# Attention rows as 64-column products on halves of TensorE's rows, all four row blocks at one place of the second layer

## The chip, the core and the metric

The kernel runs on one core of a Trainium2 chip. A core has TensorE (matrix products, with a queue PE for the products and PEld for the loads of their stationary operand), VectorE (DVE), ScalarE (ACT), GpSimd (POOL) and SyncE (SP, which here only issues DMAs). Products are written to PSUM, in eight banks of 128 partitions by 512 floats; all other tiles lie in SBUF. The metric is the time of one execution on the device in microseconds (us). Before the change the median of three runs is 261.56 us.

## What is computed

Eight batches of a linear attention are followed by one feed-forward block over all 8 x 576 tokens:

```python
kv  = einsum('bhsd,bhse->bhde', k, v)      # (8, 8, 64, 64)
out = einsum('bhsd,bhde->bhse', q, kv)     # (8, 8, 576, 64)
rms = sqrt(mean(out * out, axis=-1) + 1e-6)
x   = (out / rms * g_norm)                 # -> (4608, 512), heads side by side
h   = x @ w_in                             # (4608, 2048)
g   = h * sigmoid(1.702 * h)
y   = g @ w_out                            # (4608, 512)
```

The inputs are float32; the products take float16 operands and add up in float32.

## The kernel before

**Token tiles.** The 576 tokens of a batch are cut into 512 tokens, which make one token tile, and 64, which are collected from all batches into a ninth tile. The last loop of the kernel (line 958) runs over the nine tiles `t`. Within a tile the attention of batch `b = t + 1` is interleaved with the two layers of tile `t`. Both layers use a scheme with seven products in place of eight for a two-by-two split of the operands (`SevenIn` for the first layer, `Seven` for the second).

**The second layer.** `Seven.run` (line 670) issues the seven products in the order 1, 5, 6, 2, 7, 3, 4. Each has two row blocks (`mo`) of eight matmuls (`i`) with 256 columns: 112 matmuls, and their running number `n` is the *place* of this text. Product 1 is places 0 to 15, product 5 is 16 to 31, product 6 is 32 to 47, product 2 is 48 to 63, product 7 is 64 to 79, product 3 is 80 to 95 and product 4 is 96 to 111. Products 1, 6, 7 and 4 add up in one PSUM bank, products 5 and 3 in another, product 2 has one from the pool `ps_a`. When product 1, 5 or 6 is complete, ScalarE copies the bank to SBUF (`keep`, line 647), ahead of the next product in that bank; these are the first, second and third copy. Products 2, 7 and 3 end with an addition on VectorE (`place`, line 655), product 4 with a copy. The stationary operands of products 5, 6, 7 and 3 are sums formed on VectorE (`sums`, line 610).

**What is hung on places.** The kernel's order is written out by hand. A `Plan` lists the steps of the first layer, the sums, and at which place of the second layer each step of the attention is called (`units2`, built at lines 1021 to 1031). A step called at a place is issued right after that matmul, on whichever engines it uses, and each engine works through its own queue in that order. Tile 1 uses the plan `SECOND` (attention of batch 2); tiles 2 to 6 use `LATER` (batches 3 to 7). The plan's last products of the first layer can be left for the second: product 4 of the last part, the *late product*, is issued at place 15 in `LATER` and at place 5 in `SECOND`, with its gate on ScalarE (line 538) behind it.

**The attention of batches 2 to 7** (`class Attention`, line 210):

- `kv_product` (line 232) forms K^T V with 40 matmuls whose outputs are 64 by 64; the two heads of a pair go to the two halves of the PSUM partitions, by turns.
- `keep_kv` (line 262) copies them into `kvd`, per head pair a matrix of 128 by 128 whose two diagonal blocks hold the two halves' operands and whose other blocks are zero.
- `transpose_q` (line 270) brings q into `qTd` by a transposing DMA on SP: 128 partitions hold two token blocks of 64 head dimensions each, one above the other.
- `rows(i)` (line 303), for i = 0 to 3: four matmuls of 128 columns with `qTd` as stationary operand and the block-diagonal `kvd` as moving one, into one PSUM bank `outR`; then ScalarE squares the bank into `sq` (line 318). Each of the four banks holds two token blocks for four of the eight heads. The first three banks are from the pool `ps_h`, the fourth is from `ps_a`; there are three buffers of `sq`.
- `add_up(j)` (line 321) sums the squares over 64 columns on VectorE (line 324), `roots(h)` (line 331) takes the inverse root of two such sums on ScalarE (line 333), after a load of the activation table (line 966).
- `turn(j)` (line 335) multiplies the bank by the roots on VectorE (line 337) into `x16`, and after every second one SP issues a transposing DMA (line 346) into the next token tile's operand `xT`.
- `out`, `ss` and `apply` at the fixed places 46, 74 and 80 treat the last 64 tokens in another way: `out` has four matmuls of 64 columns (line 286).

At the start of the next tile the first layer needs `xT`, and from the fifth step on also the differences `xS` (line 490), which VectorE forms from both transposed parts.

The lines of the step that the change rewrites:

Of the kernel before, what the change touches and what calls it, by code (L numbers as in the profile page):

```python
# [7 lines left out]
F16 = mybir.dt.float16  # L8
F32 = mybir.dt.float32
ALU = mybir.AluOpType  # L10
AFT = mybir.ActivationFunctionType

P = 128
# [3 lines left out]
def kernel(  # L17
# [10 lines left out]
    nc = tc.nc  # L28

    B, H, S, D = q.shape  # L30
    DM = H * D
# [5 lines left out]
    SM = 512  # L37
    J = SM // P
# [12 lines left out]
    attn = ctx.enter_context(tc.tile_pool(name="attn", bufs=4))  # L51
# [4 lines left out]
    ps_a = ctx.enter_context(tc.tile_pool(name="ps_a", bufs=3, space=bass.MemoryType.PSUM))  # L56
    ps_h = ctx.enter_context(tc.tile_pool(name="ps_h", bufs=3, space=bass.MemoryType.PSUM))
# [88 lines left out]
    for n in "kqv":  # L146
        if n != "q":
            rows = stage.tile([P, 6, 2 * P], F32, name="qf", tag="qf", bufs=2)
            rows = rows.rearrange("p h x -> p (h x)")[0:PE_]
# [50 lines left out]


    xT = {}

    def scale_w_in(i0, i1):

        for i in (i0, HF + i0):
            w = w_in_sb[:, :, i * P : (i + i1 - i0) * P]
            nc.vector.tensor_scalar_mul(w, w, g_col)

    class Attention:  # L210
# [91 lines left out]

        def rows(self, i):

            pool, tag = (ps_h, "hT") if i < 3 else (ps_a, "att")
            t = pool.tile([P, DM], F32, name="outR", tag=tag)
            for k in range(H // 2):
                h = i % 2 * (H // 2) + k
                nc.tensor.matmul(  # L309
                    t[:, k * P : (k + 1) * P],  # L310
                    self.qTd[:, h * (J // 2) + i // 2, :],
                    self.kb[:, h // 2, :, 1 - h % 2, :],
                    start=(k == 0),
                    stop=True,
                    skip_group_check=True,
                )
            sq = attn.tile([P, SM], F16, name="sq", tag="sq", bufs=3)
            nc.scalar.activation(sq, t, AFT.Square)
            self.o[i] = (t, sq)

        def add_up(self, j):
            if j == 0:
# [10 lines left out]
            nc.scalar.activation(s4, s4, AFT.Abs_reciprocal_sqrt, bias=eps_t, scale=1.0 / D)  # L333

        def turn(self, j):
            j0, c0 = j // 2 * 2, j % 2 * (DM // 2)
            nc.vector.tensor_mul(
                self.x16[:, j0 : j0 + 2, c0 : c0 + DM // 2].rearrange("p l (h d) -> p h l d", d=D),
                self.o[j][0].rearrange("p (h l d) -> p h l d", l=2, d=D),
                self.sum4[:, j, :]  # L340
                .rearrange("p (h l) -> p h l", l=2)
                .unsqueeze(3)
                .to_broadcast([P, H // 2, 2, D]),
            )
            if j % 2:
                nc.sync.dma_start_transpose(
                    out=self.x[:, (j - 1) * KO : (j + 1) * KO, :],
                    in_=self.x16[:, j - 1 : j + 1, :].rearrange("p j n -> p (j n)"),
                )
# [407 lines left out]
    def layers(t, units1, units2):  # L757
        hid = d0 if t == 0 else Hidden(t)
        seven = Seven(t, hid.gT) if t else None
        left = hid_seven(t, hid, seven, units1) if t else first_columns(hid, units1)  # L760
        osbs[t] = opool.tile([P, 4, DM], F32, name="osb", tag="osb")
        if t:
            todo = {n: [lambda x=x: seven.sums(*x) for x in xs] for n, xs in plan(t).later.items()}
            for n, us in units2.items():
                todo.setdefault(n, []).extend(us)
            for n, us in left.items():
                todo[n] = us + todo.get(n, [])
            seven.run(todo)
        else:
            project_all(hid.gT, units2)  # L770
        if t < EARLY:
            store_early(t)
        elif t < B and t not in HALVED:
            store(t, 0, J)
# [81 lines left out]
    for hl in range(2):  # L856
        r = slice(hl * D, (hl + 1) * D)
# [34 lines left out]
    for fo in COLS[4:GROUP]:  # L892
# [25 lines left out]
        "ahoh",  # L918
        {5: '34'},
        (-1, 0, 0, 4),  # L920
        {'rows': (0, 2, 8, 19), 'add_up': (6, 26, 27, 31), 'table': 26, 'roots': (27, 33), 'turn': (40, 50, 51, 52)},
    )
    LATER = Plan(
# [7 lines left out]
        "aahh",  # L931
        {15: '34'},
        (0, 1, 6, 11),
        {'rows': (1, 1, 3, 15), 'add_up': (2, 18, 27, 22), 'table': 24, 'roots': (28, 39), 'turn': (35, 38, 46, 48)},
    )
    LAST_TWO = Plan(
# [12 lines left out]
    def plan(t):  # L949
        return SECOND if t < EARLY else LATER if t < B - 1 else LAST_TWO  # L950
# [7 lines left out]
    for t in range(NT):  # L958
        b = t + 1
        u1, u2 = {}, {}  # L960

        def at1(i, f, *args):
            u1.setdefault(i, []).append(lambda: f(*args))

        def at2(i, f, *args):
            u2.setdefault(i, []).append(lambda: f(*args))  # L966

        def of(b, name, *args):
            return lambda: getattr(live[b], name)(*args)

        if t == 0:
            for l in range(2):
                at1(6, nc.vector.memset, kvd[l], 0.0)
            at1(7, of(0, "out", NPAIR))
            at1(7, scale_w_in, 0, 4)
            at1(7, w_in_sums, 0, 2)
            at1(8, start, 1)
            at1(12, scale_w_in, 4, 6)
            at1(12, w_in_sums, 2, 3)
            at1(13, load_q, 2)  # L980
            at2(4, setattr, a0, "ss_pool", Attention.ss_pool)
            at2(4, of(0, "ss", NPAIR, True))
            at2(4, of(0, "apply", NPAIR))
            at2(18, weight_sum, 0, 0, HF)
            at2(18, scale_w_in, 6, 8)
            at2(18, w_in_sums, 3, 4)
            for c in range(NPAIR):
                at1(12, of(1, "pack_q", c))
                at2(9 + 3 * c, of(1, "q", c))
                at2((36, 37, 49, 50)[c], of(1, "kv", c))  # L990
                at2((41, 43, 54, 55)[c], of(1, "out", c))
                at2((45, 50, 58, 60)[c], of(1, "ss", c))
                at2((48, 52, 58, 62)[c], of(1, "apply", c))
            for n in range(1, 4):
                at2(19, weight_sum, n, 0, 4)
                at2(38, weight_sum, n, 4, 6)
            at2(39, load_kv, 2, 0, H // 2, False)
            at2(51, clear_rest)
            at2(51, load_kv, 2, H // 2, H)

            def first_sum():
                made[1] = Sums(1, xT[1])
                made[1].form(0)

            at2(55, first_sum)
        elif b < B:
            todo = plan(t)
            at1(todo.steps.index("kv"), of(b, "kv_all", todo.keep))
            if t == 1:
                at1(5, start, b)  # L1010
                at1(5, of(b, "transpose_q"))
                at1(4, nc.scalar.preload_act_table_set, "gelu_apprx_sigmoid_and_others")
                for n, i in ((1, 8), (2, 11), (3, 16)):
                    at1(i, weight_sum, n, 6, HF)
            if t + 2 < B:
                late = max(15, todo.steps.index("kv") + 1)
                at1(late, load_kv, t + 2)
                at1(late, load_q, t + 2)
                at2(100, start, t + 2)
                at2(100, of(t + 2, "transpose_q"))  # L1020
            at = todo.attn
            at2(at["table"], nc.scalar.preload_act_table_set, "abs_reciprocal_sqrt_and_small")
            for h in range(2):
                at2(at["roots"][h], of(b, "roots", h))
            for j in range(J):
                for name in ("rows", "add_up", "turn"):
                    at2(at[name][j], of(b, name, j))
            at2(46, of(b, "out", NPAIR))
            at2(74, of(b, "ss", NPAIR))
            at2(80, of(b, "apply", NPAIR))  # L1030
            at2(82, nc.scalar.preload_act_table_set, "gelu_apprx_sigmoid_and_others")
        elif t < B:
            for name in ("ss_pool", "rest_pool"):
                at2(16, setattr, live[1], name, (ps_a, "att"))
            at2(16, of(1, "out", NPAIR))
            at2(34, nc.scalar.preload_act_table_set, "abs_reciprocal_sqrt_and_small")
            at2(44, of(1, "ss", NPAIR))
            at2(50, of(1, "apply", NPAIR))
            at2(52, nc.scalar.preload_act_table_set, "gelu_apprx_sigmoid_and_others")
        layers(t, u1, u2)  # L1040
# [30 lines left out]
```

## Time and profile before

| | |
|---|---|
| runs of before | 261.62, 261.56, 261.07 us; median 261.56 us |
| the profiled execution | span 259.2 us from its first to its last instruction; the page gives no other time of this execution, so what lies around the span is 2.4 us against the median |
| TensorE | 251.8 us busy in products, 2500 products |
| VectorE, ScalarE, GpSimd | 194.7, 174.9, 53.6 us busy |
| granted TensorE clock | 0.998 over the span |
| row products (line 309) | 96, of which 16 belong to each of batches 2 to 7 |
| squares of the rows (line 318) | 24, 0.600 us each |
| sums of the squares (line 324) | 24, 0.679 us each |
| multiplications (line 337) | 24, 0.684 us each |

The profile is one execution seen by the hardware profiler. *Groups* gather the instructions of a line with their number, busy time and mean duration, and behind the bar the idle time of the engine just before them. *Waits* say who waited for whom, for how long and how often. The *chain of work* follows the end of the kernel back to what released each step; in order of time its rows give start, length and what ran. The *timeline* lists the instructions of an engine in order of time, equal neighbours merged. A product's duration is its latency (273 ns for 256 columns); products follow each other much closer than that.

### The profile page before, as it was taken

What the parts mean: (1) busy time and instruction counts of PE and PEld (TensorE: products, weight loads), DVE (VectorE), ACT (ScalarE), POOL (GpSimd) and SP (SyncE); (2) the same over time, 40 slices, a digit from 0 to 9 for tenths busy, and PEclk for the clock granted to TensorE, in tenths of its full rate; (3) what the DMA queues carried; (4) which work ended last, traced back from release to release, by engine and by line L of the source; (5) the groups of instructions that cost most, each with busy time, mean ns of one, the idle gap of its engine ahead of it and who ended that gap; (6) DMA issues with size and microseconds to landing.
All of it is one profiled execution on the core that took longest, in us unless ns stands there. A gap on an engine that the chain in (4) does not pass through costs nothing.

```text
span 259.2 us, 6157 instructions
## 1 busy us (share of the span) xinstructions
PE 251.8 (97%) x2500; PEld 206.3 (80%) x2500; DVE 194.7 (75%) x351; ACT 174.9 (67%) x315; POOL 53.6 (21%) x81
## 2 busy tenths in 40 slices
PE   8799999999999999999999999999999999999993
PEld 3444554788888988898889988988899888888882
DVE  1565676899968986898689958995899587557842
ACT  3477725988649964996499648974897569737820
POOL 8862245116034002500160017000000000000001
PEclk9999999999999999999999999999999999999999
DMA  7999999999999946994699799966500710021005
GB/s 174 198 202 206 204 204 196 228 188 146 201 144 193 198 78 163 153 214 71 159 105 230 102 143 157 219 82 158 154 1 12 160 73 3 0 97 68 3 0 162
DMA packets 68558, 35.31 MB, mean 136 GB/s; under 512 B 37874, under 2 KB 65778, under 8 KB 68402
## 3 DMA queue, kind: packets, MB, share of 16 engines
q0 software_dynamic: 37520, 18.17, 54.3%
q1 hardware_dynamic: 30688, 16.36, 27.5%
q8 instruction: 19, 0.31, 0.5%
q10 hardware_dynamic: 322, 0.39, 0.4%
q14 instruction: 9, 0.07, 0.1%
HBM read 36.70 MB, written 9.44 MB: 178 GB/s over the span
## 4 chain that ended last, share of the span: by engine, by line
PE 93%; POOL 2%; DMA 2%; DVE 1%; ACT 0%; issue 0%
PE h L558 38%; PE o L680 38%; PE o L794 5%; PE hT L451 5%; DMA vbuf<-in_v_dram 2%; PE outR L309 2%; PE kvp L237 2%; PE ss L357 1%; POOL qraw L90 1%; POOL kraw L90 1%; POOL vbuf L90 0%; PE kvp L249 0%; PE outT L282 0%; PE q L432 0%; DVE xT L367 0%; PE outT L286 0%
## 5 line engine op out<-in xcount | busy, mean ns | idle before, releaser
L538 ACT ACTIVATE gT<-h 128x512 f16<-128x512 f32 x96 | 52.8, 604 | 5.4 <-PE h L558 5.3
L558 PEld LDWEIGHTS <-ws 128*128 128x128 f16 x512 | 50.1, 98 | 5.8
L680 PEld LDWEIGHTS <-gS 128*128 128x128 f16 x512 | 49.7, 98 | 5.7
L558 PE MATMUL h<-xS,ws 128*128 128x256 f16 x384 | 52.2, 273 | 0.0
L680 PE MATMUL o<-tw,gS 128*128 128x256 f16 x384 | 46.3, 273 | 0.0
L558 PEld LDWEIGHTS <-w_in_sb 128*128 128x128 f16 x384 | 37.1, 98 | 4.7
L680 PEld LDWEIGHTS <-gT 128*128 128x128 f16 x384 | 37.0, 98 | 4.0
L680 PE MATMUL o<-w_out_sb,gT 128*128 128x256 f16 x256 | 33.5, 273 | 0.0
L558 PE MATMUL h<-xT,w_in_sb 128*128 128x256 f16 x224 | 31.9, 273 | 0.0
L655 DVE TENSOR_TENSOR osb<-o,qf 128x512 f32<-128x512 f32 (+1 forms) x25 | 16.7, 668 | 15.1 <-PE o L680 12.3
L572 DVE TENSOR_TENSOR h<-h,s 128x512 f32<-128x512 f32 x32 | 22.2, 697 | 6.8 <-PE h L558 5.5
L574 DVE TENSOR_TENSOR s<-h,s 128x512 f32<-128x512 f32 x32 | 22.1, 691 | 4.1 <-PE h L558 3.3
L114 POOL DMA_DIRECT2D kraw<-in_k_dram x7 | 6.0, 853 | 91.6 <-PE kvp L237 87.2
L610 DVE TENSOR_TENSOR gS<-gT 128x512 f16<-128x512 f16 (+2 forms) x32 | 21.7, 684 | 0.6 <-ACT gT L538 0.6
L538 ACT ACTIVATE gT<-s 128x512 f16<-128x512 f32 x32 | 19.8, 628 | 2.6 <-DVE s L574 2.6
L359 ACT ACTIVATE rs<-ss,eps_t 128x512 f32<-128x512 f32 (+1 forms) x16 | 9.2, 582 | 16.6 <-PE ss L357 16.5
L713 POOL DMA_DIRECT2D out_dram<-osb x2 | 1.1, 562 | 92.4 <-DVE osb L655 92.4
L558 PE MATMUL h<-xS,w_in_sb 128*128 128x256 f16 x128 | 18.9, 273 | 0.0
L966 ACT ACT_TABLE_LOAD x14 | 18.0, 1283 | 0.2
L508 ACT COPY h<-h 128x512 f32<-128x512 f32 x27 | 15.7, 585 | 2.1 <-PE h L558 2.0
L558 PE MATMUL h<-xT,ws 128*128 128x256 f16 x112 | 16.8, 273 | 0.0
L794 PE MATMUL o<-w_out_sb,gT 128*128 128x512 f16 x64 | 16.6, 380 | 0.0
(100 smaller groups left out, 367.8 us busy)
## 6 DMA issues: line engine op xcount, KB each, us to landing
out_dram<-osb SPq DMA_DIRECT2D x10, 512.0 KB, 3.1
kraw<-in_k_dram POOLq DMA_DIRECT2D x5, 512.0 KB, 7.8
vbuf<-in_v_dram POOLq DMA_DIRECT2D x5, 512.0 KB, 11.5
qraw<-in_q_dram POOLq DMA_DIRECT2D x3, 512.0 KB, 13.4
qbuf<-in_q_dram POOLq DMA_DIRECT2D x3, 512.0 KB, 12.7
out_dram<-osb SPq DMA_DIRECT2D x6, 192.0 KB, 6.1
w_in_sb<-in_moe_w_in_dram POOLq DMA_DIRECT2D x2, 512.0 KB, 10.5
w_out_sb<-in_moe_w_out_dram POOLq DMA_DIRECT2D x2, 512.0 KB, 15.1
```

The source lines that it names most:

```text
L359: nc.scalar.activation(rs[:, 0:n], t[:, 0:n], AFT.Abs_reciprocal_sqrt, bias=eps_t, scale=1.0 / D)
L451: nc.tensor.matmul(self.h[fo], w_in_sb[:, ko, fo * P : (fo + 1) * P], self.x[:, ko], start=(ko == 0), stop=(ko == KO - 1),)
L508: (nc.vector.tensor_copy if engine == "D" else nc.scalar.copy)(to, src)
L538: nc.scalar.activation(self.gT[:, to, n * TH : (n + 1) * TH], src, AFT.Gelu_apprx_sigmoid)
L558: nc.tensor.matmul(bank[name][:, a], w, x, start=(p in (1, 5) and a == 0 and k == 0), stop=(k == KH - 1), skip_group_check=True,)
L572: nc.vector.tensor_add(bank["z"], bank["x"], self.s5)
L574: nc.vector.tensor_add(self.s5, bank["x"], self.s5)
L610: op(s[:, n, lo], a, b)
L655: nc.vector.tensor_add(o, ps, self.kept[with_][:, m])
L680: nc.tensor.matmul(o, a, w, start=(p in (1, 2, 5) and i == 0 and (mo == 0 or split)), stop=(i == HF - 1), skip_group_check=True,)
L794: nc.tensor.matmul(os[mo], gT[:, fo, mo * P : (mo + 1) * P], w_out_sb[:, fo, :], start=(fo == 0), stop=(fo == FO - 1),)
L966: u2.setdefault(i, []).append(lambda: f(*args))
```

## The change

Three things change, all in the attention of batches 2 to 7.

`rows` is now called twice a batch and not four times. Each call takes two PSUM banks and issues 16 matmuls of 64 columns: for every head, one on the upper 64 rows of the array (the first token block, into the first bank) and one on the lower 64 rows (the second block, into the second bank). The zero blocks of `kvd` are no longer read by these products. Then come two squares. A bank now holds one token block for all eight heads, so `turn` writes a plain row of `x16`; it treats as many elements as before, and the transposing DMA is the same.

All 32 matmuls of a batch stand at one place: 15 in `LATER` (before: 1, 1, 3 and 15), 19 in `SECOND` (before: 0, 2, 8 and 19). In `LATER` the late product stands ahead of them.

The sums of squares move to places 17, 20, 24 and 28 in `LATER` (before: 2, 18, 27, 22) and 22, 26, 27, 31 in `SECOND` (before: 6, 26, 27, 31). The table load, the roots and the multiplications keep their places. In the order that results, ScalarE's copy of product 1 and the late product's gate come ahead of the four squares in `LATER`, where three of these squares came first.

```diff
+    ROW_BANKS = (((ps_h, "hT"), (ps_h, "hT")), ((ps_h, "hT"), (ps_a, "att")))
...
         def rows(self, i):
-            pool, tag = (ps_h, "hT") if i < 3 else (ps_a, "att")
-            t = pool.tile([P, DM], F32, name="outR", tag=tag)
-            for k in range(H // 2):
-                h = i % 2 * (H // 2) + k
-                nc.tensor.matmul(
-                    t[:, k * P : (k + 1) * P],
-                    self.qTd[:, h * (J // 2) + i // 2, :],
-                    self.kb[:, h // 2, :, 1 - h % 2, :],
-                    start=(k == 0),
-                    stop=True,
-                    skip_group_check=True,
-                )
-            sq = attn.tile([P, SM], F16, name="sq", tag="sq", bufs=3)
-            nc.scalar.activation(sq, t, AFT.Square)
-            self.o[i] = (t, sq)
+            t = [
+                pool.tile([P, DM], F32, name="outR", tag=tag)
+                for pool, tag in ROW_BANKS[i]
+            ]
+            for h in range(H):
+                for half in range(2):
+                    r = slice(half * D, (half + 1) * D)
+                    nc.tensor.matmul(
+                        t[half][:, h * D : (h + 1) * D],
+                        self.qTd[r, h * (J // 2) + i, :],
+                        self.kb[r, h // 2, half, 1 - h % 2, :],
+                        start=(h == 0),
+                        stop=True,
+                        skip_group_check=True,
+                    )
+            for half in range(2):
+                sq = attn.tile([P, SM], F16, name="sq", tag="sq", bufs=3)
+                nc.scalar.activation(sq, t[half], AFT.Square)
+                self.o[2 * i + half] = (t[half], sq)
...
         def turn(self, j):
-            j0, c0 = j // 2 * 2, j % 2 * (DM // 2)
             nc.vector.tensor_mul(
-                self.x16[:, j0 : j0 + 2, c0 : c0 + DM // 2].rearrange("p l (h d) -> p h l d", d=D),
-                self.o[j][0].rearrange("p (h l d) -> p h l d", l=2, d=D),
-                self.sum4[:, j, :]
-                .rearrange("p (h l) -> p h l", l=2)
-                .unsqueeze(3)
-                .to_broadcast([P, H // 2, 2, D]),
+                self.x16[:, j, :].rearrange("p (h d) -> p h d", d=D),
+                self.o[j][0].rearrange("p (h d) -> p h d", d=D),
+                self.sum4[:, j, :].unsqueeze(2).to_broadcast([P, H, D]),
             )
...
     SECOND = Plan(
-        {'rows': (0, 2, 8, 19), 'add_up': (6, 26, 27, 31), 'table': 26, 'roots': (27, 33), 'turn': (40, 50, 51, 52)},
+        {'rows': (19, 19), 'add_up': (22, 26, 27, 31), 'table': 26, 'roots': (27, 33), 'turn': (40, 50, 51, 52)},
...
     LATER = Plan(
-        {'rows': (1, 1, 3, 15), 'add_up': (2, 18, 27, 22), 'table': 24, 'roots': (28, 39), 'turn': (35, 38, 46, 48)},
+        {'rows': (15, 15), 'add_up': (17, 20, 24, 28), 'table': 24, 'roots': (28, 39), 'turn': (35, 38, 46, 48)},
...
             for j in range(J):
-                for name in ("rows", "add_up", "turn"):
+                if j < J // 2:
+                    at2(at["rows"][j], of(b, "rows", j))
+                for name in ("add_up", "turn"):
                     at2(at[name][j], of(b, name, j))
```

## The prediction

> **What bounds the kernel now.** I read the page's first and fourth parts first, then the waits of TensorE's two queues, then the chain of work in order of time.
>
> ```profile
> span 259.2 us, 6157 instructions
> PE 251.8 (97%) x2500; PEld 206.3 (80%) x2500; DVE 194.7 (75%) x351; ACT 174.9 (67%) x315; POOL 53.6 (21%) x81
> PE 93%; POOL 2%; DMA 2%; DVE 1%; ACT 0%; issue 0%
> ```
> ```profile
> PE idle L842 <- DVE one_t L192: 1.3, 1, 1.3
> ...
> PE hT L451 <- DVE xT L367: 0.3, 1, 0.3
> ```
>
> TensorE is the chain for 93% of the span, and the waits of its matmul queue (first and last row of four) all belong to the first token tile. From there on it runs product after product, so time saved on TensorE is time saved, unless another engine then comes late. The durations come from this one execution. Its span is 259.2 us; the median of the runs shown is 261.56, so 2.4 us lie around the span. I add differences of the span to 261.56.
>
> Now one token tile of the LATER plan (batch 3), from the chain in order of time. Columns: start, length, engine, tile, line, count; starts and ends are those of the matmuls' modelled ends.
>
> ```profile
> 86.30 0.22 PE o L680 x2
> 86.52 0.45 PE outR L309 x8
> 86.96 0.22 PE o L680 x2
> 87.18 0.22 PE outR L309 x4
> 87.40 1.31 PE o L680 x12
> 88.71 0.44 PE h L558 x4
> 89.15 0.22 PE outR L309 x4
> 89.37 3.38 PE o L680 x31
> 92.76 0.12 PE outT L286 x4
> 92.87 3.06 PE o L680 x28
> ```
>
> A product of the second layer (256 columns) takes 3.38/31 = 0.109 us. The 16 row products take 0.45 + 0.22 + 0.22 = **0.89 us** a batch, 0.056 each, and they stand without a gap among the others.
>
> **The change, part by part.**
>
> *The row products.* 16 products of 128 columns become 32 of 64 columns, each on 64 of the array's rows, upper and lower half by turns, into two PSUM banks. The trace of before has no product on half the rows. Its nearest row is the key/value product: 64 columns too, on halves of the array's columns by turns.
>
> ```profile
> 37.78 0.31 PE kvp L249 x12
> ...
> 100.95 0.75 PE kvp L237 x40
> 101.70 11.02 PE h L558 x100
> ...
> 205.80 10.91 PE h L558 x100
> ```
> ```profile
> 101.03 0.45 PE L237 MATMUL kvp<-vbuf,kraw 128*64 128x64 f16 x18
> ```
>
> The last row is the timeline of a tenth of a microsecond: 18 of these products start within 0.45 less the 0.196 us that one takes, so 9 pairs come about 0.031 us apart. Two runs of different length say the same: 20 pairs in 0.75, 6 pairs in 0.31, hence (0.75 - 0.31)/14 = 0.0314 us a pair and 0.31 - 6 x 0.0314 = 0.12 us for going in. The 100 products right behind such a run take 11.02 where 100 others take 10.91: 0.11 us for coming out. So the two halves work at the same time, and a run of halves costs 0.23 us once. With these prices a batch's rows cost 0.12 + 16 x 0.0314 + 0.11 = **0.73 us** instead of 0.89: 0.16 saved. That there is one run and not four matters: three more would cost 3 x 0.23 = 0.69 us.
>
> The bounds: if row halves do not overlap, each product costs the step of the other nearest row, L286 above (64 columns, 128-column weights): 0.12/4 = 0.029 us. Then 0.23 + 32 x 0.029 = 1.16, a loss of 0.27. If they overlap perfectly and the switch is free, 16 x 0.029 = 0.46, a saving of 0.43. I take 0.73, since the pair of L237 shares with the new one the columns, the two alternating halves, and two weight loads a pair; that the halves are rows and not columns is the untested part. The Trainium skill, TensorE: Matmul & The Clock Gate, section Packing small matmuls, says that tiles of different row groups run at the same time with starts about 4 ns apart; no row here shows it for rows.
>
> *The weight loads* double, from 16 to 32 a batch, all of 128 columns. The load record (98 ns) is a latency, since four products with such loads stand in 0.12 us in L286; a load can be had every 0.029 us. A pair needs two in 0.031 us. In L237 two loads of 64 columns fit in that time; whether two of 128 columns on separate rows do is bounded by the 1.16 above. The same page of the Trainium skill, section LDWEIGHTS (loading the stationary operand), speaks against this change: a load takes as long as its columns ask, however few rows it has, by its formula an estimated 107 ns for 128 columns, and 32 of these would be 3.4 us a batch. By that rule L286 could not stand in 0.12 us; here the trace disagrees with the figure, though not with the rule that half the rows save nothing.
>
> *The squares on ScalarE.* They move from places 1, 1, 3 of the LATER plan to 15, behind the copy of the first product and the gate of the late product. ScalarE's timeline of the same stage:
>
> ```profile
> 87.06 0.63 ACT L538 ACTIVATE gT<-s 128x512 f16<-128x512 f32 x1 [0.25 <-DVE s L574]
> 87.60 1.55 ACT L318 ACTIVATE sq<-outR 128x512 f16<-128x512 f32 x3
> 89.03 0.60 ACT L647 COPY qf<-o 128x512 f32<-128x512 f32 x1
> 89.50 0.63 ACT L538 ACTIVATE gT<-h 128x512 f16<-128x512 f32 x1
> 89.98 0.63 ACT L318 ACTIVATE sq<-outR 128x512 f16<-128x512 f32 x1
> 90.63 1.28 ACT L966 ACT_TABLE_LOAD   x1
> 91.93 0.31 ACT L333 ACTIVATE sum<-sum,eps_t 128x16 f32<-128x16 f32 x1
> 92.14 0.57 ACT L647 COPY qf<-o 128x512 f32<-128x512 f32 x1
> 92.61 0.31 ACT L333 ACTIVATE sum<-sum,eps_t 128x16 f32<-128x16 f32 x1
> 92.97 0.38 ACT L300 ACTIVATE sq<-outT 128x256 f16<-128x256 f32 x1
> 93.25 0.58 ACT L647 COPY qf<-o 128x512 f32<-128x512 f32 x1
> ```
>
> ScalarE has no gap here from 87.06 to 92.9. The new order loses it some time: after 87.69 it waits for the first product of the second layer, whose 16 parts now stand together and end at 86.30 + 16 x 0.109 = 88.05. With the steps of these rows (0.47 copy to gate, 0.48 gate to square and square to square, 0.65 to the table load, then 1.30, 0.21, 0.47, 0.36, 0.28) the copy starts at 88.09, the squares at 89.04 to 90.48, the table load at 91.13, and the third copy runs from 93.75 to **94.33**, 0.5 later than before. The squares' inputs are there in time (rows begin at 88.05 + 0.44 = 88.49). The fourth square waits for the first sum, since there are three buffers: square 0 ends at 89.65, the sum takes 0.68, 90.35 is before 90.48.
>
> Who waits for the third copy: the seventh product, which accumulates in that bank. It is place 64: the row at 92.87 begins with place 47, so place 63 ends at 92.87 + 17 x 0.109 = 94.72, and place 64 starts 0.27 before its own end, at 94.57; with 0.16 saved, 94.41. The copy is done at 94.33. So the cover is about 0.1 us, where before it was 0.74. It also caps the saving at 94.57 - 94.33 = 0.24 a batch.
>
> *VectorE.*
>
> ```profile
> 92.27 2.48 DVE L337 TENSOR_TENSOR x<-outR,sum 128x512 f16<-128x512 f32 x4
> ```
>
> The sums stand at 17 to 28 and then the four multiplications, whose elements are the same in number, only in plain order: 0.62 each as now. They shift by the same 0.5 us, to an end at 95.25. Behind them stand two transposing DMAs on SP, and the operand of the next tile. The matmul of the sums of squares (place 74, now about 95.8, then 95.6) takes a bank that the fourth multiplication frees: 0.3 us of cover. The second transposing DMA lands late in two stages already:
>
> ```profile
> DVE xS L490 <- DMA xT<-x: 2.6, 2, 1.4
> ```
>
> That wait of up to 1.4 grows by 0.5, but TensorE uses the difference formed from it only after 8 products, the key/value run and 4 more, 0.87 + 0.86 + 0.44 = 2.2 us into the tile. I cost it at nothing; without that cover it would be 0.5 in two stages. SP has nothing else to issue ahead of these DMAs. DMAs, bytes and the loads on POOL are unchanged.
>
> *Batch 2, the SECOND plan.*
>
> ```profile
> 59.67 0.69 DVE L574 TENSOR_TENSOR s<-h,s 128x512 f32<-128x512 f32 x1
> ...
> 61.81 1.55 DVE L610 TENSOR_TENSOR gS<-gT 128x2048 f16<-128x2048 f16 x2
> ```
> ```profile
> L680 PEld LDWEIGHTS <-gS 128*128 128x128 f16 x2 | 0.1, 98 | 0.1
> ```
>
> The second row's sums end at 63.36, and the group of loads in the 0.12 us behind that has 0.1 us of idle time: the load of place 22 waits for them today already. VectorE gets there through work that the change doesn't touch, so place 22 can't come earlier, and batch 2 saves **nothing**. TensorE would also meet the late product 0.07 before its input (60.36 + 0.04, against 60.33). With these, place 20 could start early by 0.1 at most; the wait swallows it.
>
> **Sum:** 5 batches x 0.16 = 0.8, with 0.18 if the switch is a little cheaper than its rounded rows: 0.8 to 0.9. 261.56 - 0.86 = **260.7 us**.
>
> **The rivals.**
>
> 1. *The halves take turns* (the change doesn't do what it says): two loads, or two results for the same 128 PSUM partitions, can't go at once. For it: no row shows row halves, and loads double. Against it: L237's pairs. It decides from a pair of (0.89 - 0.23)/16 = 0.041 us upward. Price: 0.27 in each of 5 batches; in batch 2, place 20 would follow 14 products and 1.16 of rows behind the late product's end at 61.0: 63.69 for 63.37, 0.32. In all +1.7: **263.2 us**, slower. If a load cost more than 0.029, still slower; the far end is 32 loads at their full record of 98 ns, 3.1 us a batch and some 14 us in all, which the L286 row makes unlikely. The formula of the Trainium skill's page named above would give 3.4 - 0.89 = 2.5 us a batch, an estimate that lies close to that far end.
>
> 2. *ScalarE takes back what TensorE gains*: the third copy comes some 0.2 later than I count (the multi-wait in front of the fourth square, the first sum late), and the seventh product waits for it. The cover is 0.1 against an error of a similar size in eleven summed steps. Each tenth beyond it costs 0.1 in five batches, and the whole saving is gone at 0.26. Time: 261.1 to 261.8, **261.5 us**. A pair of 0.036 to 0.045 us ends in the same place.
>
> **How the numbers follow.** Forecast (halves overlap, cover holds) 0.52; ScalarE or a slow pair eats the gain 0.18; halves take turns 0.30, of which 0.05 for loads dearer than 0.029. A measurement of this kernel can tell about 0.2%, 0.5 us, from no change; the forecast lies beyond that, rival 2 mostly within. Faster 0.52, same 0.18, slower 0.30. The forecast's own range is 260.3 (the cap: 5 x 0.24) to 261.0. The range must take in rival 1 at 263.2 and leaves out the dear loads: 260.2 to 263.4.
>
> **What would show it.** In the chain of after, one run of 32 row products of about 0.62 us a batch with 0.1 behind it; in the timeline, pairs 0.03 us apart; the stage from one first product to the next shorter by 0.16 in batches 3 to 7 and not in batch 2; no waits of TensorE for the third copy. Single steps of 0.029 or more in that run show rival 1; a wait of the seventh product for the third copy (line 647 of before) shows rival 2. I am wrong as well if a stall appears at the start of the next tile, behind the transposing DMAs.

## The result, and the profile after

The changed kernel's median is **260.35 us** (20 runs), that of the kernel before 261.38 us (20 runs in the same stretch of time). The ratio of the runs is 0.9958, with a 95% interval of 0.9945 to 0.9970: 0.4%, or 1.1 us, faster (0.8 to 1.4 us). The prediction was 260.7 us. Executions that took 1.7 to 4.7 times as long as the others (one each in three of the experiments) count in no ratio, and where the profiled one was among them the kernel was profiled once more under a second name.

First the head of the page after.

```profile
span 258.8 us, 6349 instructions
...
PE 251.4 (97%) x2596; PEld 203.7 (79%) x2596; DVE 195.1 (75%) x351; ACT 174.9 (68%) x315; POOL 53.8 (21%) x81
```

There are 96 products more, and yet TensorE is busy 0.4 us less. The two profiled spans differ by only 0.4 us and the runs by 1.1. The chain says why. In order of time (start, length, engine, tile, line, count) it has for the start of token tile 1 before:

```profile
57.12 2.73 PE h L558 x24
...
75.27 11.02 PE h L558 x100
```

and for tile 1 and the first of the LATER tiles after:

```profile
57.88 2.73 PE h L559 x24
...
76.02 11.02 PE h L559 x100
87.04 1.75 PE o L681 x16
...
89.22 0.57 PE outR L313 x32
89.80 3.49 PE o L681 x31
...
93.40 3.06 PE o L681 x28
...
102.23 11.02 PE h L559 x100
```

The profiled execution of the changed kernel reached tile 1 0.76 us later (57.88 against 57.12). That is ahead of the first changed product, so it is a difference of two start-ups and not of the change. From there on we count tile by tile, from one group of 24 or 100 first-layer products to the next. Tile 1 takes 76.02 - 57.88 = 18.14, before 75.27 - 57.12 = 18.15: nothing saved. A LATER tile takes 102.23 - 76.02 = 26.21, before 101.70 - 75.27 = 26.43: **0.22 us saved**, and there are five of them, 1.1 us. That is what the runs show. (259.2 + 0.76 - 0.01 - 1.1 = 258.8, the span.)

Where the 0.22 comes from stands in the same rows. The 32 row products are one piece of 0.57 us; the 31 products behind it take 3.49 where the same 31 took 3.38 before, so 0.11 for coming out. Together 0.68 us, where the 16 products of before took 0.89. Within the piece, the starts of single products in the trace, in us, are these (first eight and last six of 32):

```
89.155 89.158 89.194 89.197 89.223 89.227 89.252 89.256 ... 89.544 89.547 89.573 89.576 89.602 89.606
```

Two products start 3 to 4 ns apart, one for each half of the rows, and pairs follow each other every **0.029 us** (14 steps from 89.194 to 89.602). The Trainium skill (TensorE: Matmul & The Clock Gate, section Packing small matmuls) gives about 4 ns for such starts; this trace bears it out. A product lasts 0.190 us and a load 0.095, each much longer than the step, as the rows of line 313 say (duration in ns: least, median, most):

```profile
L313 PEld LDWEIGHTS <-qTd x192: 92/95/97, 63.2 to 194.4; 64*128 64x128 f16 x192
L313 PE MATMUL outR<-kvd,qTd x192: 189/190/201, 63.2 to 194.5; 64*128 64x64 f16 x192
```

So two loads of 128 columns on separate rows are had every 0.029 us, the time of one such load over all rows.

The waits of TensorE's load queue after have two rows to look at.

```profile
PEld L238 <- issue: 1.3, 6, 0.2
PEld L313 <- issue: 1.3, 6, 0.2
...
PEld L681 <- DVE gS L611: 0.3, 1, 0.3
```

At each of the six entries into such a run the load queue stands idle for 0.2 us with no releaser in the profile, exactly as at the key/value run of line 238. That goes with the switch to halves: in the kernel with the new order and full-row products (below) no such row stands for its row products. The switch costs 0.68 - 16 x 0.029 = 0.22 in all. The last row is new: one load waits for VectorE's sums. It is in batch 2, the timeline of the load queue says where:

```profile
63.21 0.52 PEld L313 LDWEIGHTS <-qTd 64*128 64x128 f16 x32 [0.21 <-issue]
63.78 0.11 PEld L681 LDWEIGHTS <-gS 128*128 128x128 f16 x2
64.16 0.88 PEld L681 LDWEIGHTS <-gS 128*128 128x128 f16 x9 [0.26 <-DVE gS L611]
```

Behind the row run at place 19 come the loads of places 20 and 21, then 0.26 of idle time until the second row's sums are there. Batch 2 did gain its 0.2 on the products and gave most of it back within 1 us. The rest, 0.06, it had lost ahead of the run: the late product stands there, TensorE now reaches it before VectorE has its input ready, and its four matmuls take 0.50 in the chain, before 0.44.

Last, ScalarE in a LATER tile, its timeline after:

```profile
88.82 0.58 ACT L648 COPY qf<-o 128x512 f32<-128x512 f32 x1 [0.39 <-PE o L681]
...
89.79 2.08 ACT L323 ACTIVATE sq<-outR 128x512 f16<-128x512 f32 x4
...
93.86 0.31 ACT L338 ACTIVATE sum<-sum,eps_t 128x16 f32<-128x16 f32 x1
94.07 0.37 ACT L301 ACTIVATE sq<-outT 128x256 f16<-128x256 f32 x1
94.33 0.58 ACT L648 COPY qf<-o 128x512 f32<-128x512 f32 x1
```

The first row is the first copy, which now waits for the whole of product 1. Behind it come the gate of the late product, the four squares without a gap, the second root, the square of `outT`, and the third copy, which ends at 94.91. Counted from the tile's first second-layer product (87.04) that is 7.87 us; before it was 93.83 - 86.30 = 7.53. Product 7 starts at 95.10: place 47 begins behind 93.40, so 17 products end at 95.26, and the next starts 0.273 ahead of its own end at 95.37. The copy is 0.19 us early. TensorE does not wait for it.

### The profile page after: what moved, and what is told of

It reads as the page before. It is cut to its first block, busy times and chain, and to the rows that moved or that the text cites. A ratio compares the mean times of both kernels' runs of the same rounds, so it can differ in the third digit from the quotient of the medians.

```text
span 258.8 us, 6349 instructions
## 1 busy us (share of the span) xinstructions
PE 251.4 (97%) x2596; PEld 203.7 (79%) x2596; DVE 195.1 (75%) x351; ACT 174.9 (68%) x315; POOL 53.8 (21%) x81
## 4 chain that ended last, share of the span: by engine, by line
PE 92%; DMA 4%; DVE 1%; issue 0%; ACT 0%; POOL 0%
PE o L681 38%; PE h L559 38%; PE o L795 6%; PE hT L452 5%; DMA qraw<-in_q_dram 2%; DMA vbuf<-in_v_dram 2%; PE kvp L238 2%; PE outR L313 1%; PE ss L358 1%; PE kvp L250 0%; PE outT L283 0%; PE q L433 0%; DVE xT L368 0%; PE outT L287 0%; ACT rs L360 0%
## 5 line engine op out<-in xcount | busy, mean ns | idle before, releaser
L681 PEld LDWEIGHTS <-gT 128*128 128x128 f16 x384 | 37.6, 98 | 4.3
L681 PE MATMUL o<-w_out_sb,gT 128*128 128x256 f16 x256 | 31.4, 273 | 0.0
L648 ACT COPY qf<-o 128x512 f32<-128x512 f32 (+1 forms) x26 | 14.2, 547 | 4.5 <-PE o L681 4.3
L329 DVE TENSOR_REDUCE sum<-sq 128x8 f32<-128x512 f16 x24 | 15.3, 678 | 2.5 <-ACT sq L323 2.5
```

What stands on the lines that cost most here:

```text
L329: nc.vector.tensor_reduce(out=self.sum4[:, j, :], in_=self.o[j][1].rearrange("p (x d) -> p x d", d=D), op=ALU.add, axis=mybir.AxisListType.X,)
L648: nc.scalar.copy(self.kept[as_][:, m], ps)
L681: nc.tensor.matmul(o, a, w, start=(p in (1, 2, 5) and i == 0 and (mo == 0 or split)), stop=(i == HF - 1), skip_group_check=True,)
```

## The experiments

The theory behind the prediction (A): the halves of the rows work at the same time when they come by turns, a run costs 0.2 us to enter and leave, and all of the gain is that run. The rivals were that the new order alone brings it (B), that a second run costs nothing (C), that the turns don't matter (D), and that ScalarE and VectorE have more, or less, time to spare than I read. Ratios are against the kernel before in the same stretch of time; the changed kernel's is 0.9958.

**The order alone.** The kernel before, with its 128-column products and square tiles, but in the places of the change:

```diff
-        {'rows': (0, 2, 8, 19), 'add_up': (6, 26, 27, 31), 'table': 26, 'roots': (27, 33), 'turn': (40, 50, 51, 52)},
+        {'rows': (19, 19, 19, 19), 'add_up': (22, 26, 27, 31), 'table': 26, 'roots': (27, 33), 'turn': (40, 50, 51, 52)},
...
-        {'rows': (1, 1, 3, 15), 'add_up': (2, 18, 27, 22), 'table': 24, 'roots': (28, 39), 'turn': (35, 38, 46, 48)},
+        {'rows': (15, 15, 15, 15), 'add_up': (17, 20, 24, 28), 'table': 24, 'roots': (28, 39), 'turn': (35, 38, 46, 48)},
```

> The kernel before with its 128-column products, but with all four row blocks at place 15 (LATER) and 19 (SECOND) and the sums of squares at the places of the changed kernel: the order without the halves. Theory A (the gain is the halves at work at the same time): 16 products of 0.056 still cost 0.89 us a batch, and no wait goes: 0.0 against before, within 0.3 us. Rival B (the gain is the order: rows, copy and gate at other places): about 1.0 us faster than before, as the changed kernel.

Measured: 261.42 us, ratio 1.0017 (0.9999 to 1.0034). The same kernel's second profile:

> [...] Theory A: one run of 16 products of 128 columns a batch in the chain, 0.89 us without anything for going in and out, the stage of a LATER tile 26.43 us as before, and no wait of TensorE for the third copy.

Its chain:

```profile
77.16 11.02 PE h L558 x100
...
90.36 0.89 PE outR L309 x16
91.26 3.38 PE o L680 x31
...
103.59 11.02 PE h L558 x100
```

0.89 for the rows as before, no 0.11 behind them (3.38), and a tile of 103.59 - 77.16 = 26.43, to the hundredth that of before. (This one execution took 262.71 us beside 261.91 of the kernel before. Its tile 1 began at 58.96, in the profile of before at 57.12, and the five LATER tiles are as long as there: the difference lies ahead of them.) The order brings nothing by itself: B falls.

**Two runs in place of one.** The changed kernel with its 32 products split again, 16 at place 1 and 16 at place 15, the sums of squares moved with them:

```diff
-        {'rows': (15, 15), 'add_up': (17, 20, 24, 28), 'table': 24, 'roots': (28, 39), 'turn': (35, 38, 46, 48)},
+        {'rows': (1, 15), 'add_up': (2, 18, 22, 27), 'table': 24, 'roots': (28, 39), 'turn': (35, 38, 46, 48)},
```

> The changed kernel with the first call of rows at place 1 in LATER and the second at 15, sums of squares at 2, 18, 22, 27 as before: the halves in two runs a batch. Theory A (a run of halves costs about 0.2 us once for going in and out): 2 x 0.2 + 16 x 0.029 = 0.87 a batch, nearly the 0.89 of before, so 0.0 to 0.2 us faster than before and 0.9 to 1.0 slower than the changed kernel. Rival C (going in and out costs nothing, or is hidden by the load of weights): as the changed kernel, 1.0 us faster than before.

Measured: 261.36 us, ratio 0.9999 (0.9987 to 1.0011). The chain of one tile:

```profile
75.86 11.02 PE h L559 x100
...
87.10 0.34 PE outR L313 x16
87.44 1.64 PE o L681 x14
...
89.51 0.34 PE outR L313 x16
...
102.29 11.02 PE h L559 x100
```

Both runs pay: 0.34 for 8 pairs is 8 x 0.029 = 0.23 and 0.11 for going in, and the 14 products behind the first run take 1.64 where 14 x 0.109 = 1.53. The tile is 26.43 long, as before the change. The second run costs 0.22 and eats the whole gain: C falls. That all 32 products stand at one place is no ornament of the change: in two runs the halves win nothing.

**No turns within a call.** The same 16 products of a call, eight for the upper half and then eight for the lower one:

```diff
-            for h in range(H):
-                for half in range(2):
+            for half in range(2):
+                for h in range(H):
```

> The changed kernel with the two loops of rows exchanged: eight products on the upper rows, then eight on the lower ones, so that neighbours use the same rows and cannot overlap. Theory A (a pair overlaps because neighbours are on different rows): 32 x 0.029 + 0.2 = 1.13 instead of 0.67 a batch, 0.46 more in each of five batches; in batch 2 the wait of 0.26 at place 22 takes up part, 0.2 more; 2.5 us slower than the changed kernel, 1.5 slower than before. Rival D (a 64-row product is simply half as dear, whatever its neighbour): as the changed kernel, 1.0 us faster than before.

Measured: 261.26 us, ratio 0.9996 (0.9986 to 1.0007), that is 0.0038 or 1.0 us more than the changed kernel. Neither theory had this number: A without turns wanted 2.5, D nothing. The chain:

```profile
76.96 11.02 PE h L559 x100
...
90.17 0.74 PE outR L313 x32
...
103.35 11.02 PE h L559 x100
```

The run takes 0.74, and the tile 26.39: 0.18 more than in the changed kernel, not 0.5. The starts of the products around the first two turns tell more (us, from the trace):

```
90.103 90.141 90.171 90.200 90.229 90.237 90.258 90.276 90.287 90.306 90.316 90.335 90.364 90.372 90.393 90.411 90.422 90.440 90.451 90.469
```

These are three series, each with one step of 0.038 or 0.039 us behind its first product and steps of 0.029 from there on: 90.103, 90.141 and so on to 90.316, the upper half's eight; 90.237, 90.276 and so on to 90.451, the lower half's eight, which begin while three upper ones (90.258, 90.287, 90.316) are still to come; and 90.372, 90.411, 90.440, 90.469 and on, the next call's upper half, which begins with three lower ones (90.393, 90.422, 90.451) to come. The records don't name the half, but they have its end: the eighth of each series, at 90.316 and at 90.451, carries the signal that its bank is complete, and in the program the one at 90.316 stands ahead of the one at 90.237. So TensorE does overlap the halves at a turn, and it starts products of the other half ahead of up to three that stand before them in the program. New theory (G): it looks ahead by some three products, so at each turn some three pairs overlap and the rest goes one by one at 0.029.

**One turn in all.** All 16 products of the upper half, then all 16 of the lower one, into four banks, and then the four squares (the second call issues nothing):

```diff
+            if i:
+                return
...
-                for pool, tag in ROW_BANKS[i]
+                for banks in ROW_BANKS
+                for pool, tag in banks
...
-            for h in range(H):
-                for half in range(2):
+            for half in range(2):
+                for n in range(2):
+                    for h in range(H):
...
-                        t[half][:, h * D : (h + 1) * D],
-                        self.qTd[r, h * (J // 2) + i, :],
+                            t[2 * n + half][:, h * D : (h + 1) * D],
+                            self.qTd[r, h * (J // 2) + n, :],
...
```

> The changed kernel with all 16 products on the upper rows first and then all 16 on the lower ones (four banks at once): one turn between halves where the variant with loops exchanged has three a batch and the changed kernel 31. Theory G (TensorE looks ahead: a product for the other half of the rows starts before some 3 queued ones of the first half, so each turn overlaps 3 to 4 products, whatever the neighbours): one turn saves 3 to 4 x 0.029 = 0.1, the run takes about 0.95 us in the chain instead of 0.57 (changed) and 0.74 (three turns); 0.38 more in five batches and 0.12 in batch 2, 2.0 us slower than the changed kernel, 1.0 slower than before. Theory D (a 64-row product is cheaper by itself): 0.74 as with three turns, 0.9 slower than the changed kernel.

Measured: 262.45 us, ratio 1.0034 (1.0018 to 1.0050), 0.0076 or 2.0 us more than the changed kernel. The chain:

```profile
76.22 11.02 PE h L563 x100
...
89.42 0.94 PE outR L317 x32
...
102.80 11.02 PE h L563 x100
```

A run of 0.94, a tile of 26.58 (0.37 more than the changed kernel, five times 1.85, and 0.2 in tile 1). The single starts show one turn with three products overtaken (a lower one at 89.723, upper ones still to come at 89.744, 89.773, 89.802). The three runs are one rule: 32 products by 0.029, less 0.029 for each overlapped pair, and some 0.1 to get in. 16 pairs: 0.46 + 0.11 = 0.57. Three turns of three: 23 steps, 0.67 + 0.1 = 0.77 (0.74 measured). One turn: 29 steps, 0.84 + 0.1 = 0.94. The changed kernel's turns pay 0.94 - 0.57 = 0.37 us a batch; without them the change would have been a loss. D falls. G holds with a number of about three; why it is three no run here shows.

**Batch 2: the sums earlier.** The changed kernel with one other place: the sums for product 7, which nobody needs soon, are called at place 6 and not at 4, and so stand on VectorE's queue behind the sums that place 22 waits for:

```diff
-        {0: ((0, 4, 3),), 4: ((0, 8, 2),), 26: ((4, 8, 1),), 72: ((4, 8, 3),)},
+        {0: ((0, 4, 3),), 6: ((0, 8, 2),), 26: ((4, 8, 1),), 72: ((4, 8, 3),)},
```

> The changed kernel with the sums for product 7 in SECOND called at place 6 instead of 4, so that VectorE forms the last sums for product 5 first. Theory A (batch 2 saves nothing because place 22 waits for those sums): the wait of 0.26 of TensorE's load for VectorE goes, but the third copy on ScalarE then ends 0.16 to 0.2 after product 7 is ready, and a wait for it appears; in all 0.05 to 0.1 us faster than the changed kernel, too little for the runs, to be seen in the waits. Rival E (place 22 waits for something else, or nothing follows): 0.26 us faster than the changed kernel, without a new wait.

Measured: 260.22 us, ratio 0.9958 (0.9944 to 0.9972). The wait behind the row run is gone, and tile 1 is 75.78 - 57.68 = 18.10, 0.04 shorter. The rest of the 0.2 went to a wait that I had not named. The timeline of the load queue and that of VectorE:

```profile
63.59 1.64 PEld L681 LDWEIGHTS <-gS 128*128 128x128 f16 x16
65.43 1.10 PEld L681 LDWEIGHTS <-gS 128*128 128x128 f16 x11 [0.20 <-DVE gS L611]
```
```profile
64.09 0.69 DVE L329 TENSOR_REDUCE sum<-sq 128x8 f32<-128x512 f16 x1 [0.17 <-ACT sq L323]
64.70 0.68 DVE L611 TENSOR_TENSOR gS<-gS,gT 128x1024 f16<-128x1024 f16 x1
```

Sixteen loads further (place 36), product 6 needs a sum that stands on VectorE behind the first sum of squares, and this one waits for a square, since with the rows at place 19 the squares come late. I had expected a wait for the third copy. The total came out near the forecast (0.04 by the tile, for 0.05 to 0.1), the reason did not.

**Batch 2: the rows earlier too.** The kernel of the last experiment, and besides the rows of batch 2 at place 15, so that the squares come earlier as well:

```diff
-        {'rows': (19, 19), 'add_up': (22, 26, 27, 31), 'table': 26, 'roots': (27, 33), 'turn': (40, 50, 51, 52)},
+        {'rows': (15, 15), 'add_up': (22, 26, 27, 31), 'table': 26, 'roots': (27, 33), 'turn': (40, 50, 51, 52)},
```

> The variant with the sums for product 7 called at place 6, and besides with the rows of SECOND at place 15 instead of 19, so that the squares, the first sum of squares and the sums for product 6 behind it come 0.25 to 0.3 us earlier. Theory A (batch 2's saving waits for VectorE, first at place 22, then at place 36 behind the first sum of squares): no wait of TensorE for VectorE is left in batch 2, which saves 0.22 to 0.26 us, 0.1% against the changed kernel, to be seen in the waits rather than in the runs. Rival E (another wait takes its place, for the third copy or for the fourth multiplication): no gain against the changed kernel and a new row in the waits.

Measured: 260.22 us, ratio 0.9957 (0.9939 to 0.9974). Its chain in tile 1:

```profile
57.62 2.73 PE h L559 x24
...
61.00 0.49 PE h L559 x4
...
62.59 0.57 PE outR L313 x32
63.16 3.49 PE o L681 x31
...
75.60 11.02 PE h L559 x100
```

The 31 products behind the run take 3.49, as in a LATER tile: no wait is left in them. Tile 1 is 17.98 long, 0.17 shorter than before the change and 0.16 shorter than in the changed kernel, where the forecast was 0.22 to 0.26. The row at 61.00 has the rest: the late product still takes 0.49 there, before the change 0.44. So batch 2 has the gain in it too, less that 0.05, and VectorE's order held it back. 0.17 us is 0.07% and too little for the runs: this version and the changed kernel are not told apart by time, only by the trace.

**How much time ScalarE has left.** In batches 3 to 7 the third square is done twice, which is repeated work only:

```diff
             for half in range(2):
                 sq = attn.tile([P, SM], F16, name="sq", tag="sq", bufs=3)
                 nc.scalar.activation(sq, t[half], AFT.Square)
+                if self.b > EARLY and i == 1 and half == 0:
+                    nc.scalar.activation(sq, t[half], AFT.Square)
```

> The changed kernel with one more square in each of batches 3 to 7 (the third square is done twice), so that ScalarE's third copy ends 0.48 us later. Theory A (rival 2 of the prediction as a mechanism: the third copy has a cover of 0.19 us in the changed kernel, and beyond it product 7 waits): a wait of 0.3 us of TensorE for the copy in each of five batches, 1.5 us slower than the changed kernel, 0.4 slower than before. Rival F (the copy has more cover than that, the squares are off the path): as the changed kernel, 1.0 us faster than before.

Measured: 262.61 us, ratio 1.0049 (1.0033 to 1.0065), 0.0091 or 2.4 us more than the changed kernel. The same kernel's second profile:

> [...] The runs gave 2.3 us more than the changed kernel instead of 1.5. Theory A as it was: the third copy ends 0.48 later and product 7 waits 0.3 for it, five times. Theory H (a second wait behind it: the roots and multiplications are late as well, and a matmul that needs the fourth multiplication's bank, or the next tile's operand, waits again): 0.3 at product 7 and 0.1 to 0.2 more at the matmul of place 74 or at the start of the next tile.

First its waits of TensorE, then rows of its chain, which now runs over ScalarE in this stage, then of ScalarE's timeline:

```profile
PE o L683 <- ACT qf L650: 1.7, 5, 0.3
```
```profile
75.22 11.02 PE h L561 x100
86.24 1.76 PE o L683 x16
...
94.80 1.36 PE o L683 x11
...
101.93 1.09 PE h L561 x9
```
```profile
89.00 1.58 ACT L323 ACTIVATE sq<-outR 128x512 f16<-128x512 f32 x3
90.61 0.60 ACT L325 ACTIVATE sq<-outR 128x512 f16<-128x512 f32 x1
...
94.16 0.58 ACT L650 COPY qf<-o 128x512 f32<-128x512 f32 x1
```

The seventh product waits for the third copy in all five batches: rival 2 of the prediction, made to happen. No other wait of TensorE for an engine appeared, so a second one (H) falls. Two sizes differ from the forecast. The third copy ends 94.74 - 86.24 = 8.50 into the tile, 0.63 later than in the changed kernel and not 0.48: the repeated square writes the buffer that the third has just written, and starts only when that is complete, at 90.61 behind 89.00 + 1.58. And the tile is 101.93 - 75.22 = 26.71 long, 0.50 more than 26.21, though the row of waits shows 1.7/5 = 0.34 of idle time. The row at 94.80 tells why: 11 products in 1.36 = 0.273 + 10 x 0.109. Behind a wait the first product's latency stands alone, where otherwise all but 0.109 of it lies under its forerunner; 0.273 - 0.109 = 0.16 is the difference. So the changed kernel had 0.63 - 0.50 = **0.13 us** to spare in front of product 7.

## Why the prediction was right, point by point

**The row products.** Right in mechanism, and the one untested part (rows in place of columns) held. Predicted 0.73 us a batch, measured 0.68; saved 0.16 predicted, 0.22 measured. The mis-sized term is the step of a pair: 0.0314 us, taken from the column halves, is 0.029 between row halves; 16 x 0.0024 = 0.04. The 0.12 for going in and 0.11 for coming out, read from the key/value run, stood within 0.015 (0.57 - 0.46 and 3.49 - 3.38). The saving was put at 0.86 us and is 1.1 by the trace; the rest of the distance from 260.7 to 260.35 lies in the median of before, 261.56 in the three runs that the sum started from and 261.38 in these twenty.

**One run and not four.** Argued from the price of 0.23; the two-run kernel measured 0.22 for one more.

**The weight loads.** Right: two loads of 128 columns on separate rows in one step. What each load costs by itself stayed hidden, as it was for line 286 before.

**ScalarE.** Predicted: the third copy 0.5 later, 0.1 to spare. Measured: 0.34 later, 0.13 to spare (by the fifth-square kernel; 0.19 by the ends alone). The step that failed is the 0.36 from the second root to the square of `outT`: in the trace of before this step held a wait for `outT`, which came in at 92.88. In the new order that product is long there, and the step takes 94.07 - 93.86 = 0.21. (It was some 0.36 in all five LATER tiles before, but 0.21 in tile 1, where `outT` was there 0.4 us ahead of the square.) A step read off a timeline can have a wait in it that the new order drops. The order of the chain and each other step stood to 0.02. The predicted 0.08 between the two ends became 0.08 + 0.16 for the earlier copy - 0.05 for the earlier product 7 = 0.19, of which 0.06 goes between a copy's end and the product that waited for it (94.74 to 94.80 in the fifth-square kernel): 0.13. That the 0.1 of the forecast came out so near is luck: without the 0.16 that was costed too much, the other two (0.05 and 0.06) would have taken all of the 0.08.

**VectorE.** The multiplications start 6.48 us into the tile (93.52 - 87.04), before 5.97: 0.5 later, as predicted, and nothing on TensorE waits. Two rows of VectorE's timeline after (the first sum of squares now waits 0.47 for its square, which was there in time before):

```profile
90.43 1.28 DVE L329 TENSOR_REDUCE sum<-sq 128x8 f32<-128x512 f16 x2 [0.47 <-ACT sq L323]
...
93.52 2.48 DVE L341 TENSOR_TENSOR x<-outR,sum 128x512 f16<-128x512 f32 x4
```

One thing went the other way: the wait of the differences for the second transposing DMA, which I let grow by 0.5, shrank.

```profile
DVE xS L491 <- DMA xT<-x: 1.2, 2, 0.7
```

It was 2.6 in 2 before. It was costed at nothing and is off the path in both kernels, so the time doesn't hang on it; why the DMA landed sooner behind later multiplications wasn't tried and stays open.

**Batch 2.** Predicted nothing, measured 0.01, for the reasons given: place 22 waits for the second row's sums, and TensorE meets the late product before its input, which costs 0.06, where 0.07 was read from the rows. The two kernels with other places show that the first of them is order and not work: 0.17 was to be had.

**Rival 1** (the halves take turns, 263.2) is excluded for this order of products by the pairs 3 to 4 ns apart. The one-turn kernel comes near to it (262.45): there 29 of 32 steps are single ones. **Rival 2** (261.5) is real in its mechanism and its place, and its threshold was not reached: another 0.13 us on ScalarE, and it takes what the products gave.

## What to carry to other kernels

Before you halve small products onto parts of the array, look for any run of halves in the trace and read three prices from it: the step of a pair, going in, and coming out; here 0.029, 0.11 and 0.11 us, so that 16 pairs in one run win 0.2 us and the same pairs in two runs win nothing. Issue the halves by turns and all in one run, and then ask of each engine that feeds the products behind them how early it is now: here ScalarE had 0.13 us left in five tiles, and VectorE none in the sixth, where the saving vanished until its queue was put in another order. When a wait is expected, add to its idle time the part of the product's latency that no longer overlaps, 0.16 us here.

## What the runs showed of the hardware that was not expected

- TensorE started products for one half of the rows ahead of up to three earlier ones for the other half, at every turn read above (a lower one at 90.237, upper ones at 90.258, 90.287 and 90.316). The Trainium skill, TensorE: Matmul & The Clock Gate, section Packing small matmuls, says that products start strictly in the order of the program. Read by their series, the starts and the signals of the kernel without turns in a call disagree, and so do the starts of the one-turn kernel; those of the changed kernel, which alternates, can't tell.
- Row halves are a little faster than column halves with the same 64 columns of output: 0.029 us a pair against 0.0314, though they load twice as many columns a pair. One product of 64 columns over all the rows takes the same 0.029 (line 287, four in 0.12 us), so on the halves of the rows the second product of a pair came free.
